# Fifteen matmuls that nothing reads, a load moved behind the weights and a unit moved between two steps, at the start of a Fourier filter with a mixture of experts

## The chip, the core and the metric

The kernel runs on one core of a Trainium2 chip. A core has a matrix engine (TensorE, PE in the rows), a vector engine (VectorE, DVE), a scalar engine (ScalarE, ACT), a general engine (GpSimd, POOL) and a sync engine (SyncE, SP), which here does little but start transfers; 16 DMA engines carry the transfers. The metric is the time of one execution in microseconds, as the median of several runs; less is better.

## What is computed

For each of 8 sequences of 3136 rows and 256 columns: a real Fourier transform along the rows, a complex 256 x 256 matrix with a bias, a shrinking of small values to zero, the transform back; then, on the result, the 128 rows with the highest score go through a two-layer network whose output is added to them. Cut to what matters:

```python
X = np.fft.rfft(x, axis=1)
Yr = X.real @ w_r - X.imag @ w_i + b_r
Yi = X.real @ w_i + X.imag @ w_r + b_i
Yr = np.sign(Yr) * np.maximum(np.abs(Yr) - 0.01, 0.0)   # Yi likewise
y = np.fft.irfft(Yr + 1j * Yi, n=3136, axis=1)
for b in range(8):
    top = np.argpartition(-(y[b] @ w_gate), 128)[:128]
    ye = np.maximum(y[b, top] @ w1, 0.0) @ w2
    out[b, top] = y[b, top] + sigmoid(y[b, top] @ w_gate)[:, None] * ye
```

## The kernel before

The transform of length 3136 is split as 49 x 64, and so is every batch's work.

- **First stage**, `s1(b, i)`, i from 0 to 7 (a unit): a load of 512 KB of x (`ld_x`), four matmuls of 49 x 64 on 512 columns each that fill the four quarters of the array, and two copies out, one on ACT (L430), one on DVE (L431). For b > 0 the result goes to DRAM as `As[b]` (512 KB). Batch 0 is split: the even rows of each unit go to `early` (256 KB, `st_a(i, 0)`), the odd rows later to `late` (`st_a(i, 1)`).
- **Second stage**, `s2(b, g)`, g from 0 to 12 (a step of a batch): four matmuls of 128 x 128 on the tile `av` and the constants `g_sb` into the one PSUM buffer `px`; then `Xh`, `Xl`, a split of the result in two parts, by ACT (L466, L467), DVE (L468) and POOL (L469). `ld_a` loads `av` from `early`, `late` or `As` for two steps at a time in two transfers of 256 KB.
- **Spectral stage**, `spectral(b, g, p)`: twelve matmuls of 256 columns for each p of 0 and 1 (L221 to L223), then the shrinking (L490, L492, L497) and a split (L504, L505).
- **Back**: `s2i`, a store of its result, `ld_c`, `s1i`, and the score and network in threads between the steps.

The main loop runs over t, the count of steps of all batches. Step t does, in this order on TensorE, `s2` of step t+1, the first half of `spectral` of step t, `s2i` of step t-2, the second half, and then units of `s1` of later batches where the list `first` has them due: units 2 and 3 of batch 1 in step 2, 4 and 5 in step 4. `s2` of batch 0 is written (0,0), (0,1) and so on below.

Order is fixed by hand: `ordered` ties each instruction to the one before it on PE, ACT, DVE and SP; `ld` ties each load on SP to the load before it (`queued`). So an instruction on TensorE that waits holds up all that stand behind it there, and the transfers that SP starts go out in the order of the program. `flush` starts the stores that have gathered since the last step.

Ahead of the main loop stands a part of its own: the eight loads of batch 0, the eight units with their stores to `early`, one load and unit of batch 1, the weights `w_r` and `w_i` with their split (`split_w`), the first `av`, the second load of batch 1, further constants, and the stores to `late`. Its unit (1,1) stands in step 0 of the loop, behind `s2` (0,1).

Of the kernel before, what the change touches and what calls it, by code (L numbers as in the profile page):

```python
# [10 lines left out]
F32 = mybir.dt.float32  # L11
# [6 lines left out]
ALU = mybir.AluOpType  # L18

B, S, D = 8, 3136, 256  # L20
# [85 lines left out]
def fourier_moe(ctx: ExitStack, tc: tile.TileContext, x, w_r, w_i, bri, wg, w1, w2,  # L106
                t_wf, t_wq, t_g, t_gi, t_m, t_dig, outs, cap):
    nc = tc.nc
# [3 lines left out]
    pool = ctx.enter_context(tc.tile_pool(name="work", bufs=2))  # L112
    ps = ctx.enter_context(tc.tile_pool(name="ps", bufs=2, space=bass.MemoryType.PSUM))
# [6 lines left out]
    def c_tile(shape, dt, name):  # L120
        return const.tile(shape, dt, name=name)

    w1f, w1tf = c_tile([128, 64], F32, "w1f"), c_tile([128, 64], F32, "w1tf")
    w1p = c_tile([128, 64], F32, "w1p")
    nc.scalar.dma_start(out=w1p, in_=t_wf[2])
    nc.scalar.dma_start(out=w1f, in_=t_wf[0])
    early, late = [dram.tile([2, 32, N2, 128], F32, name=n, bufs=1) for n in ("early", "late")]
    last = {}
    g_sb = c_tile([128, NJ, 128], F32, "g_sb")
# [19 lines left out]
    def queued(eng, f):  # L149
        if eng in last:  # L150
            with tc.issue_after(last[eng]):
                last[eng] = f().ins
        else:
            last[eng] = f().ins

    def ld(out, src):
        queued(nc.sync, lambda: nc.sync.dma_start(out=out, in_=src))
# [4 lines left out]
    def ld_w(src, name, bufs):  # L162
        t = pool.tile([128, 2, D], F32, name=name, bufs=bufs)
        ld(t, src.rearrange("(h p) e -> p h e", p=128))
        return t

    def split_w(t, h, l):
        nc.vector.tensor_copy(h, t)
        nc.vector.tensor_tensor(out=l, in0=t, in1=h.bitcast(F32), op=ALU.subtract)

    def add_bias():
        nc.vector.tensor_scalar(out=bias, in0=bias, scalar1=LAM, scalar2=None, op0=ALU.add)
        nc.vector.memset(m2l, -2.0 * LAM)

    def consts_g(k):
        s = slice(4 * k, min(4 * k + 4, NJ))
        ld(g_sb[:, s, :], t_g[:, s, :])

    def ld_gi(k):
        s = slice(4 * k, min(4 * k + 4, NJ))  # L180
        t = pool.tile([P, 8, 128], F32, name="cv", bufs=4)[:, :s.stop - s.start, :]
        ld(t, t_gi[:, s])
        gis.append((t, s))
# [7 lines left out]
    def consts_b():  # L191
        ld(wq, t_wq)
        ld(w1tf, t_wf[1])
        make_identity(nc, ident)
# [205 lines left out]
    def store(dst, src):  # L400
        if t < ORD:
            nc.sync.dma_start(out=dst, in_=src)
        else:
            stores.append((dst, src))

    def flush():
        for dst, src in stores:
            nc.sync.dma_start(out=dst, in_=src)
        stores.clear()
        done["s1i"] = done["last"]  # L410

    def tiles4(out, w, src):
        for r in (1, 0):
            for c in range(2):
                last_mm = nc.tensor.matmul(out[r][64 * c:64 * c + 64], w[64 * r:64 * r + N1, :], src(r, c), start=True, stop=True)  # L415
        return last_mm.ins

    def ld_x(b, i):
        xt[b, i] = pool.tile([P, 4, D], F32, name="cv" if b == 0 and i >= 4 else "xt", bufs=4)
        ld(xt[b, i], x[b, i])  # L420

    def s1(b, i):
        if i == 0:
            As[b] = dram.tile([2, 64, N2, 128], F32, name="As")
        n = ("at", "at", "at", "ct", "ct", "ot", "ot", "ot")[i] if b == 0 else "cv" if b == 1 and i < 2 else "at"
        a = pool.tile([P, 8, 128], F32, name=n, bufs={"ct": 2, "cv": 4}.get(n, 3))
        p = [ps.tile([P, 4, 128], F32, name="s", bufs=4) for _ in range(2)]
        xi = xt.pop((b, i))
        tiles4(p, w1f if b else w1p, lambda r, c: xi[64 * r:64 * r + N1, :, 128 * c:128 * c + 128])
        nc.scalar.copy(out=a[:, :4, :], in_=p[0])  # L430
        nc.vector.tensor_copy(a[:, 4:, :], p[1])  # L431
        if b > 0:
            store(As[b].rearrange("h q n d -> (h q) n d")[:, 8 * i:8 * i + 8, :], a)
        else:
            made.append(a)
# [3 lines left out]
    def st_a(i, k):  # L439
        ld((early, late)[k].rearrange("h q n d -> (h q) n d")[:, 8 * i:8 * i + 8, :], made[i][k::2])  # L440

    def pads(h):
        ld(As[0][h, N1:].rearrange("p (i n) d -> i p (n d)", n=8), x[0, :, 64 * h + N1:64 * h + 64].rearrange("i p m d -> i p (m d)"))
# [126 lines left out]
    PE, ACT, DVE, SP = [getattr(mybir.EngineType, n) for n in ("PE", "Activation", "DVE", "SP")]  # L570
# [65 lines left out]
    def ordered(f, *args, engines=()):  # L636
        bb = nc.cur_bb.bb.instructions
        n = len(bb)
        f(*args)
        for i in bb[n:]:  # L640
            if i.engine in (engines or (PE, ACT, DVE, SP)):
                if i.engine in chain:
                    tc.add_manual_dep(i, chain[i.engine].name, mybir.DependencyInfo(
                        mybir.DependencyClass.NoSync, mybir.DependencyReason.DATA), reason="main order")
                chain[i.engine] = i

    def at_step(u, f, n, kind=None):
        if 0 <= u < B * G:
            for i in range(-(-(u * n) // G), -(-((u + 1) * n) // G)):
                if t < ORD:  # L650
                    f(*divmod(i, n))
                else:
                    ordered(f, *divmod(i, n))
                if kind and i % n == n - 1:
                    done[kind] = i // n
# [7 lines left out]
    def to_step(u, f):  # L663
        todo = unloaded if f is ld_c else left
        while len(todo) > B * U - units_by(u):
            b, i = todo[0]
            ordered(f, b, i)
            if f is s1i and i == U - 1:
                done["last"] = b
# [7 lines left out]
    def firsts(u):  # L677
        for i in first:
            if first[i] == u:
                ordered(s1, *divmod(i, U))  # L680

    def loads(u):
        for n in range(1 if u < 0 else U):
            i = loaded[0]
            if u < -AP or i == B * U or first[i] > u + XP or sum(first[k] >= u for k in range(U + 2, i)) > 3:
                break
            ordered(ld_x, *divmod(i, U))
            loaded[0] += 1

    t = -1  # L690
    for i in range(U):
        ld_x(0, i)
    consts_g(0)
    for i in range(U):
        s1(0, i)
        st_a(i, 0)
        if i == 1:
            ld_x(1, 0)
    ws = [ld_w(w_r, "r1", 1), ld_w(w_i, "Yl", YB)]
    s1(1, 0)  # L700
    split_w(ws[0], wrh, wrl)
    split_w(ws[1], wih, wil)
    ld_a(0, 0)
    ld_a(0, 1)
# [12 lines left out]
    for t in range(-1, B * G):  # L717
        if t > 0:
            at_step(t + AP, ld_a, G)
        loads(t)  # L720
        to_step(t + 2, ld_c)
        if t < ORD:
            flush()
        else:
            ordered(flush)
        if t >= 0 and t % 2 == 0 and (t + 4) // 2 in range(2, 7):
            consts_g((t + 4) // 2)
        if t % 2 and (t + 3) // 2 in range(2, 7):
            ld_gi((t + 3) // 2)
        if t == 10:  # L730
            consts_b()
        if t in (14, 16):
            pads((t - 14) // 2)
        if t in range(20, 20 + 2 * (FF // 128 + 2), 2):
            consts_moe((t - 20) // 2)
        at_step(t + 1, s2, G)
        if t == 0:
            ordered(s1, 1, 1)
            add_bias()
        at_step(t - 1, shrink_c, G)  # L740
        tick(threads)
        at_step(t, lambda b, g: spectral(b, g, 0), G)
        if t == B * G - 1:
            at_step(t, shrink_a, G)
            at_step(t, shrink_b, G)
            at_step(t, shrink_c, G)
        at_step(t - 2, s2i, G)
        if t == B * G - 1:
            at_step(t - 2, gate, G, "s2i")
            break  # L750
        at_step(t, lambda b, g: spectral(b, g, 1), G)
        at_step(t, shrink_a, G)
        firsts(t)
        at_step(t - 2, gate, G, "s2i")
        at_step(t, shrink_b, G)
        if t < B * G - 2:
            to_step(t, s1i)
        if t == 0 or t % 2 and (t + 1) // 2 in range(1, 7):
            ordered(consts_gi, *gis.pop(0))
        if t in range(28, 28 + 2 * (FF // 128), 2):  # L760
            ordered(split_w2, (t - 28) // 2)
        tick(threads)
        if main_pe[0] is not None:
            with tc.issue_after(main_pe[0]):
                ticks[0] += 1
                tick(ffns)
# [80 lines left out]
```

## Time and profile before

| | us |
|---|---|
| median of 3 runs | 702.11 |
| lowest and highest of them | 702.02, 702.75 |
| profiled execution, its own time | 703.28 |
| profiled execution, span from first to last instruction | 701.5 |

The rows further down come from the one profiled execution: its 703.28 us are 701.5 of span and 1.8 around it. Times in rows are counted from the first instruction. PE is busy 670.2 us of the span. A matmul of 128 x 256 in fp32r takes one record, one in f32 two; a unit of `s1` gives 8 records, `s2` of a step gives 8. TensorE's clock has two levels, 1.2 and 2.4 GHz; PEclk 0.50 is the first and 1.00 the second. The row of PEclk says 1.00 from the span's start on, before its first change is recorded.

### The profile page before, as it was taken

The numbers are of one execution on the slowest core, as the hardware profiler recorded it, in microseconds if no ns is written. First come the engines' busy times: TensorE is split into PE (matmuls) and PEld (weight loads), VectorE is DVE, ScalarE is ACT, GpSimd is POOL, SyncE is SP. The second block draws the span as 40 slices with busy tenths as digits, with TensorE's granted clock in tenths as the row PEclk, the third lists the DMA queues.
The fourth block names the chain that finished last, engine by engine and source line by source line (L and its number), as shares of the span: only waits on it lengthen the run. The fifth ranks groups of instructions, "written<-read, shape, count | busy, mean of one in ns | idle before, by whom it ended". The sixth has DMA issues, their size and how long they took to land.

```text
span 701.5 us, 15027 instructions
## 1 busy us (share of the span) xinstructions
PE 670.2 (96%) x5482; PEld 552.9 (79%) x5482; DVE 464.8 (66%) x1330; ACT 384.3 (55%) x759; POOL 209.5 (30%) x255
## 2 busy tenths in 40 slices
PE   6499999999999999999999999999999999998997
PEld 2288888989888988888888798788878888876666
DVE  2355666666665555555877877777997789866852
ACT  2255665655566666666566556655555454445441
POOL 1034342233333333222223232322323222232321
PEclk9699999999999999999999999999999999999999
DMA  9999987787799999999899999887778665647950
GB/s 334 310 370 376 324 269 254 250 282 248 259 346 340 332 329 317 338 309 334 283 333 329 304 321 333 279 308 256 240 217 254 207 214 186 198 154 217 388 229 23
DMA packets 146791, 196.31 MB, mean 280 GB/s; under 512 B 8725, under 2 KB 111278, under 8 KB 146718
## 3 DMA queue, kind: packets, MB, share of 16 engines
q1 hardware_dynamic: 145518, 193.08, 81.8%
q0 software_dynamic: 912, 2.21, 1.0%
q8 instruction: 43, 0.70, 0.4%
q14 instruction: 30, 0.25, 0.1%
q10 hardware_dynamic: 288, 0.07, 0.0%
HBM read 101.59 MB, written 94.83 MB: 280 GB/s over the span
## 4 chain that ended last, share of the span: by engine, by line
PE 79%; DVE 11%; issue 4%; DMA 3%; ACT 2%; POOL 0%; SPq 0%; POOLq 0%; DVEq 0%; ACTq 0%
PE s L415 16%; PE px L463 12%; PE py L221 12%; PE py L222 12%; PE py L223 12%; PE s L221 3%; PE s L222 3%; PE s L223 3%; DMA av<-early 2%; DVE py L490 2%; DVE junk L536 2%; DVE yf L497 1%; PE py L369 1%; DVE Xl L468 1%; PE s L369 1%
## 5 line engine op out<-in xcount | busy, mean ns | idle before, releaser
L505 POOL TENSOR_TENSOR Yl<-yf,Yh 128x512 fp32r<-128x512 f32 (+1 forms) x104 | 130.6, 1255 | 331.6 <-ACT Yh L504 325.4
L492 ACT ACTIVATE r<-py,m2l 128x512 f32<-128x512 f32 (+1 forms) x104 | 69.8, 672 | 169.7 <-DVE py L490 165.1
L490 DVE TENSOR_TENSOR py<-py,bias 128x512 f32<-128x512 f32 (+1 forms) x104 | 70.3, 676 | 110.6 <-PE py L223 105.4
L463 PEld LDWEIGHTS px<-g_sb,av 128*128 128x128 f32 (+1 forms) x800 | 99.3, 194 | 40.2 <-DVE at L431 21.3
L463 PE MATMUL px<-g_sb,av 128*128 128x128 f32 (+1 forms) x800 | 114.7, 286 | 9.3 <-DMA av<-early 7.0
L221 PE MATMUL py<-wrh,Xh 128*128 128x256 f32 x400 | 122.2, 306 | 0.0
L223 PE MATMUL py<-wrl,Xh 128*128 128x256 f32 x400 | 112.7, 282 | 0.0
L222 PE MATMUL py<-wrh,Xl 128*128 128x256 f32 x400 | 112.6, 282 | 0.0
L221 PE MATMUL py<-wih,Xh 128*128 128x256 f32 x400 | 112.4, 281 | 0.0
L222 PE MATMUL py<-wih,Xl 128*128 128x256 f32 x400 | 112.1, 280 | 0.0
L223 PE MATMUL py<-wil,Xh 128*128 128x256 f32 x400 | 111.8, 279 | 0.0
L468 DVE TENSOR_TENSOR Xl<-px,Xh 128x512 fp32r<-128x512 f32 (+1 forms) x104 | 69.5, 668 | 34.0 <-ACT Xh L467 26.8
L536 DVE CUSTOM_DVE_ANT_0 junk<-ct,wgb 128x256 f32<-128x256 f32 (+1 forms) x200 | 86.5, 433 | 6.1 <-ACT ct L523 2.9
L523 ACT COPY ct<-s 128x512 f32<-128x512 f32 (+1 forms) x104 | 59.3, 571 | 51.6 <-PE s L223 50.2
L221 PEld LDWEIGHTS py<-wrh,Xh 128*128 128x128 f32 x400 | 75.9, 190 | 3.5 <-issue 2.3
L222 PEld LDWEIGHTS py<-wrh,Xl 128*128 128x128 f32 x400 | 76.0, 190 | 0.9 <-issue 0.9
L223 PEld LDWEIGHTS py<-wrl,Xh 128*128 128x128 f32 x400 | 75.8, 189 | 0.0
L221 PEld LDWEIGHTS py<-wih,Xh 128*128 128x128 f32 x400 | 75.5, 189 | 0.0
L222 PEld LDWEIGHTS py<-wih,Xl 128*128 128x128 f32 x400 | 75.4, 188 | 0.0
L223 PEld LDWEIGHTS py<-wil,Xh 128*128 128x128 f32 x400 | 75.3, 188 | 0.0
L466 ACT CAST Xh<-px 128x512 fp32r<-128x512 f32 (+1 forms) x104 | 59.6, 573 | 27.7 <-PE px L463 22.0
L497 DVE SCALAR_TENSOR_TENSOR yf<-py,r 128x512 f32<-128x512 f32 (+1 forms) x104 | 69.4, 668 | 6.6 <-ACT r L492 2.3
(129 smaller groups left out, 1201.1 us busy)
## 6 DMA issues: line engine op xcount, KB each, us to landing
xt<-in_x SPq DMA_DIRECT2D x60, 512.0 KB, 6.7
cv<-As SPq DMA_DIRECT2D x58, 512.0 KB, 5.5
out<-ot SPq DMA_DIRECT2D x57, 512.0 KB, 3.8
As<-at SPq DMA_DIRECT2D x54, 512.0 KB, 4.0
As<-ct SPq DMA_DIRECT2D x96, 256.0 KB, 4.7
av<-As SPq DMA_DIRECT2D x84, 256.0 KB, 4.9
out<-at SPq DMA_DIRECT2D x7, 512.0 KB, 7.7
xt<-As SPq DMA_DIRECT2D x6, 512.0 KB, 4.1
```

Of the source, the lines that this page charges most:

```text
L221: nc.tensor.matmul(out, wh, mh, start=start, stop=False)
L222: nc.tensor.matmul(out, wl, mh, start=False, stop=False)
L223: return nc.tensor.matmul(out, wh, ml, start=False, stop=stop).ins
L415: last_mm = nc.tensor.matmul(out[r][64 * c:64 * c + 64], w[64 * r:64 * r + N1, :], src(r, c), start=True, stop=True)
L463: nc.tensor.matmul(px[:, 2 * p + h, :], a[:, h, 2 * (g % 2) * (w - 1) + p, :], g_sb[:r, 2 * g + p, :], start=True, stop=True)
L466: nc.scalar.copy(out=xh[:, :, NF:], in_=px)
L468: nc.vector.tensor_tensor(out=xl[:, :, NF:], in0=px, in1=xh[:, :, NF:].bitcast(F32), op=ALU.subtract)
L490: nc.vector.tensor_tensor(out=p, in0=p, in1=bias[:, :w, :], op=ALU.add)
L492: nc.scalar.activation(out=r1[b, g], in_=p, func=AF.Relu, bias=m2l, scale=1.0)
L497: nc.vector.scalar_tensor_tensor(out=yf, in0=py.pop((b, g)), scalar=0.0, in1=r1.pop((b, g)), op0=ALU.min, op1=ALU.add)
L505: nc.gpsimd.tensor_tensor(out=yl, in0=yf, in1=yh.bitcast(F32), op=ALU.subtract)
L536: nc.vector.tensor_tensor_reduce(out=junk[:r], in0=c[:, k, :], in1=wgb[:r], scale=1.0, scalar=0.0, op0=ALU.mult, op1=ALU.add, accum_out=Cs ...
```

## The change

- `w1f`, the first-stage constant of batches 1 to 7 (32 KB), is loaded on SP behind the loads of batch 0 and `g_sb`, and not on ACT's queue at the start.
- A tile `busy` is filled with 0.5 by DVE, and four f32 matmuls of 128 x 256 on it stand ahead of batch 0's units on TensorE, eleven more behind them. Their result is read by nothing.
- The units of batch 0 and unit (1,0) are tied in order on TensorE.
- The load of unit (1,0) moves from behind batch 0's second store to behind the weights.
- The low parts of the split weights are made by POOL, and not DVE.
- Unit (1,1) moves from step 0 to step -1, between `s2` (0,0) and `s2` (0,1); its store is then in the next `flush`, one step earlier.
- `add_bias` is tied in order.

```diff
-    nc.scalar.dma_start(out=w1f, in_=t_wf[0])
...
     def split_w(t, h, l):
         nc.vector.tensor_copy(h, t)
-        nc.vector.tensor_tensor(out=l, in0=t, in1=h.bitcast(F32), op=ALU.subtract)
+        nc.gpsimd.tensor_tensor(out=l, in0=t, in1=h.bitcast(F32), op=ALU.subtract)
...
     consts_g(0)
+    ld(w1f, t_wf[0])
+    busy = pool.tile([128, 2, D], F32, name="yf")
+    nc.vector.memset(busy, 0.5)
+    unread = ps.tile([128, 2, 128], F32, name="m", bufs=1)
+
+    def keep_clock(n):
+        for _ in range(n):
+            nc.tensor.matmul(unread, busy[:, 0, :128], busy[:, 1, :].rearrange("p (a c) -> p a c", a=2), start=True, stop=True)
+
+    ordered(keep_clock, 4, engines=(PE,))
     for i in range(U):
-        s1(0, i)
+        ordered(s1, 0, i, engines=(PE,))
         st_a(i, 0)
-        if i == 1:
-            ld_x(1, 0)
+    ordered(keep_clock, 11, engines=(PE,))
     ws = [ld_w(w_r, "r1", 1), ld_w(w_i, "Yl", YB)]
-    s1(1, 0)
+    ld_x(1, 0)
+    ordered(s1, 1, 0, engines=(PE,))
...
         at_step(t + 1, s2, G)
+        if t < 0:
+            ordered(s1, 1, 1)
         if t == 0:
-            ordered(s1, 1, 1)
-            add_bias()
+            ordered(add_bias)
```

Where instructions stand now. On TensorE, from the start to the first spectral stage, before (`m` is the PSUM tile of the unread matmuls, `s` that of a unit, `px` that of `s2`, `py` that of `spectral`):

```order
L415 MATMUL s<-xt,w1p 64x512 x16
L415 MATMUL s<-cv,w1p 64x512 x16
L415 MATMUL s<-xt,w1f 64x512 x4
L463 MATMUL px<-g_sb,av 128x128 x8
L415 MATMUL s<-xt,w1f 64x512 x4
L221 MATMUL py<-wrh,Xh 128x256
```

and in the change:

```order
L700 MATMUL m<-yf 128x256 x4
L414 MATMUL s<-xt,w1p 64x512 x16
L414 MATMUL s<-cv,w1p 64x512 x16
L700 MATMUL m<-yf 128x256 x11
L414 MATMUL s<-xt,w1f 64x512 x4
L462 MATMUL px<-g_sb,av 128x128 x4
L414 MATMUL s<-xt,w1f 64x512 x4
L462 MATMUL px<-g_sb,av 128x128 x4
L220 MATMUL py<-wrh,Xh 128x256
```

Unit (1,1), the second `s<-xt,w1f`, has moved between the two `s2`, and the unread matmuls stand around batch 0's 32.

On SP, from the constants behind batch 0's loads to the first `av`, before:

```order
L157 DMA g_sb<-t_g 128x512
L157 DMA early<-at 64x1024 x2
L157 DMA xt<-in_x 128x1024
L157 DMA early<-at 64x1024
L157 DMA early<-ct 64x1024 x2
L157 DMA early<-ot 64x1024 x3
L157 DMA r_193<-in_w_r 128x2x256
L157 DMA Yl<-in_w_i 128x2x256
L157 DMA av<-early 128x4x128 x2
```

and in the change:

```order
L156 DMA g_sb<-t_g 128x512
L156 DMA w1f<-t_wf 128x64
L156 DMA early<-at 64x1024 x3
L156 DMA early<-ct 64x1024 x2
L156 DMA early<-ot 64x1024 x3
L156 DMA r_209<-in_w_r 128x2x256
L156 DMA Yl<-in_w_i 128x2x256
L156 DMA xt<-in_x 128x1024
L156 DMA av<-early 128x4x128 x2
```

One load of x, 512 KB, has moved behind six stores and the weights; the number of bytes ahead of `av` is the same but for `w1f`.

On SP some 25 transfers later, around the third pair of `av`, which is for `s2` (0,4) and (0,5); `As<-cv` is the store of a unit of batch 1. Before:

```order
L157 DMA xt<-in_x 128x1024
L408 DMA As<-cv 128x1024
L157 DMA xt<-in_x 128x1024 x3
L157 DMA g_sb<-t_g 128x512
L157 DMA av<-early 128x4x128 x2
L408 DMA As<-cv 128x1024
L157 DMA cv<-t_gi 128x512
```

and in the change:

```order
L156 DMA xt<-in_x 128x1024
L407 DMA As<-cv 128x1024
L156 DMA xt<-in_x 128x1024 x3
L407 DMA As<-cv 128x1024
L156 DMA g_sb<-t_g 128x512
L156 DMA av<-early 128x4x128 x2
L156 DMA cv<-t_gi 128x512
```

The store of unit (1,1) has moved ahead of a constant and the pair of `av`. Behind this place the order of every engine is that of before.

## Rows read from the trace of the kernel before

**Rows 1.** The page: busy time by engine, and the chain that ended last, by engine.

```profile
PE 670.2 (96%) x5482; PEld 552.9 (79%) x5482; DVE 464.8 (66%) x1330; ACT 384.3 (55%) x759; POOL 209.5 (30%) x255
...
PE 79%; DVE 11%; issue 4%; DMA 3%; ACT 2%; POOL 0%; SPq 0%; POOLq 0%; DVEq 0%; ACTq 0%
```

**Rows 2.** That chain in order of time, 0 to 60 us: start, us, what.

```profile
5.62 13.19 PE s L415 x64
...
19.44 3.51 DMA early<-ot
23.15 3.99 DMA av<-early
...
31.26 2.07 PE px L463 x8
33.33 1.92 PE s L415 x8
...
35.76 0.21 PE py L222
...
37.41 0.12 PE py L221
...
41.77 8.22 DMA av<-early
```

**Rows 3.** TensorE in order of time: start, us, what [idle before it, and releaser].

```profile
27.27 2.30 PE L463 MATMUL px<-g_sb,av 128*128 128x128 f32 x8 [6.84 <-DMA av<-early]
...
39.00 1.05 PE L463 MATMUL px<-g_sb,av 128*128 128x128 f32 x8
...
47.33 1.95 PE L415 MATMUL s<-xt,w1f 49*64 49x512 f32 x16
...
50.03 0.94 PE L463 MATMUL px<-g_sb,av 128*128 128x128 f32 x6 [0.17 <-DMA av<-early]
...
527.48 0.18 PE L271 MATMUL m<-n,tm 128*128 128x6 bf16 x1 [1.58 <-DVE idx L338]
```

**Rows 4.** Stretches: us, busy PE, PEld, DVE, ACT, POOL; PEclk, DMA share, GB/s.

```profile
23.00:24.00 1.00, 0.00 (x0) 0.00 (x0) 0.00 (x0) 0.00 (x0) 0.00 (x0) 0.77 0.21 73
24.00:25.00 1.00, 0.00 (x0) 0.00 (x0) 0.43 (x2) 0.00 (x0) 0.00 (x0) 0.50 0.59 178
...
37.00:38.00 1.00, 1.00 (x10) 1.00 (x9) 0.00 (x0) 0.00 (x0) 0.00 (x0) 0.90 1.03 395
...
49.00:50.00 1.00, 0.73 (x6) 0.30 (x2) 0.83 (x3) 0.95 (x2) 0.00 (x0) 1.00 1.04 404
```

**Rows 5.** VectorE in order of time, the copies out of batch 0's units.

```profile
14.46 0.69 DVE L431 COPY ct<-s 128x512 f32<-128x512 f32 x1 [1.01 <-PE s L415]
16.17 0.69 DVE L431 COPY ot<-s 128x512 f32<-128x512 f32 x1 [1.02 <-PE s L415]
17.39 0.69 DVE L431 COPY ot<-s 128x512 f32<-128x512 f32 x1 [0.53 <-PE s L415]
18.25 0.69 DVE L431 COPY ot<-s 128x512 f32<-128x512 f32 x1 [0.17 <-PE s L415]
```

**Rows 6.** SP in order of time: start, us, what it issues.

```profile
10.65 0.54 SPq L157 DMA_DIRECT2D xt<-in_x  x1
...
41.20 1.22 SPq L157 DMA_DIRECT2D av<-early  x2
42.53 1.76 SPq L408 DMA_DIRECT2D As<-cv  x1
```

**Rows 7.** All transfers from 36 to 50 us.

```profile
DMA packets 2617, 5.24 MB, mean 374 GB/s; under 512 B 228, under 2 KB 1307, under 8 KB 2617
```

**Rows 8.** The page's costliest groups: a subtraction of 128 x 512 on POOL.

```profile
L505 POOL TENSOR_TENSOR Yl<-yf,Yh 128x512 fp32r<-128x512 f32 (+1 forms) x104 | 130.6, 1255 | 331.6 <-ACT Yh L504 325.4
```

**Rows 9.** Stretches at the end, PE alone: us, busy PE, PEclk, DMA share, GB/s.

```profile
696.00:697.00 1.00, 0.77 (x7) 1.00 0.00 0
...
699.00:700.00 1.00, 0.00 (x0) 0.69 0.37 131
```

## The prediction

> **What bounds the kernel now.** I read the page first: PE is busy 96% of the span and holds 79% of the chain that ended last, DMA only 3% of it [rows 1]. So the end is set by how early TensorE gets into its unbroken work, and what a change at the start is worth is read from where the chain last leaves TensorE for something else. I then followed the chain in order of time [rows 2]. It goes through batch 0's units (13.19 us), the last store to `early` (19.44, 3.51 us to land), the first `av` (23.15, 3.99 us), `s2`, unit (1,1) and the first spectral matmuls, and then once more through a transfer: the pair of `av` whose second half was issued at 41.77 and took 8.22 us, up to 49.99. TensorE's own rows say the same: the last six records of `s2` (0,4) start at 50.03 and waited for `av` [rows 3]. The 3% of DMA in the chain, some 21 us, are the pieces up to here and the first load; behind 50 us no transfer is on the chain. The reader should see from this that there are two stretches: up to 50.03 the DMA queue decides, behind it TensorE's own work, 651.5 us of the 701.5.
>
> The clock is the third thing. PEclk falls in the stretch 23 to 24 us, mean 0.77, is 0.50 in the next, and comes back in 37 to 38, mean 0.90 [rows 4]. The spectral matmul at 35.76 takes 0.21 us of the chain, the one at 37.41 takes 0.12 [rows 2]. In the first stage the profile prints 1.00, but the copies out of the units follow each other after 1.71 us (14.46 to 16.17) and later after 0.86 us (17.39 to 18.25) [rows 5]: the first units ran at the low level too, until 16 or 17 us.
>
> **The change part by part.**
>
> *Unread matmuls.* The trace has none. The nearest row is `s2`: four f32 matmuls of 128 columns in 1.05 us at 39.00 and in 2.30 us at 27.27 [rows 3], so 256 columns cost 0.53 us at the high and 1.15 at the low level. Four ahead of batch 0 cost 2.1 to 4.6 us; they begin behind a fill of 128 x 512 on DVE, which I price as a copy, 0.69 us [rows 5], and TensorE's first matmul waits until 5.62 anyway [rows 2]. They are hidden, or push the first unit by some 0.3 us. Eleven behind it cost 5.8 to 12.6 us. TensorE stands still there for 6.84 us before `s2` (0,0) [rows 3]; at the high level they fit. At the low level they would run over by up to 6 us, and what hides that is the wait at 50 us, below.
>
> *First stage at the high clock, if the four raise it.* Eight units at 0.86 rather than 1.71 us are paced by the arrival of x. The last store to `early` is then issued up to 2 us before 19.44. It lands no earlier than the queue in front of it lets it.
>
> *Load of (1,0).* It leaves its place at 10.65 [rows 6], ahead of six stores to `early`, and goes behind the weights, ahead of `av`. One transfer of 512 KB (0.524 MB) at the 374 GB/s of a full queue [rows 7] is 1.40 us. So the stores can land up to 1.40 us earlier. But as many bytes as before go ahead of `av`, so `av` gains only what the queue stood idle: 0.79 us in 23 to 24 and 0.41 in 24 to 25 [rows 4], together **1.20 us**. Ends: 0 if the last store is issued no earlier (its 3.51 us stay), 1.40 if the whole transfer comes off. I take 1.20, since the idle stretch is a row and the moved load is what fills it. Every transfer behind `av` is issued in a full queue and gains the same.
>
> *Weights' low parts on POOL.* Two subtractions at 1.26 [rows 8], 2.5 us in a row, where DVE took two of 128 x 512 at about 0.69 each: 1.1 us more. The weights stand ahead of `av` in the queue, and the first spectral matmul comes 3.8 us or more behind `av`, so `s2` covers it: nothing. Without that cover it would be 1.1 us on TensorE, again inside the wait at 50 us.
>
> *w1f on SP, `add_bias` tied.* 32 KB in the queue is 0.09 us, and `w1f` is needed only at unit (1,0). The bias is ready long before its use. Nothing.
>
> *Unit (1,1) between the steps, with a clock kept up.* `s2` (0,1) starts 1.69 us after `s2` (0,0) ends (27.27 + 2.30 to 31.26), because `px` must be emptied. The unit fits into that: half of 1.95 [rows 3]. At the high level TensorE does `s2` (1.05), waits 1.69 with the unit in it, and does `s2` (1.05): 3.8 us from the landing of `av` to the first spectral matmul, where it now takes 8.0 (27.27 to 33.33 + 1.92). I allow 1.5 us for x of (1,1), which lands behind `av`; then TensorE is 1.2 + 8.0 - 5.3 = 3.9 us ahead, and the nine spectral matmuls up to 37.2 that took 0.21 rather than 0.12 give 0.8 more: **4.7 us ahead**.
>
> *What is late next.* `s2` (0,4). Its `av` is issued in a full queue (DMA share 1.03 and 1.04 in the stretches on either side, [rows 4]), so it lands when the bytes ahead of it are through. These are 1.20 us earlier, but the store of (1,1), issued at 42.53 behind this `av` [rows 6], now stands ahead of it: another 512 KB, **1.40 us**, later. Net: 49.99 - 1.20 + 1.40 = 50.19. TensorE arrives 4.7 us early, near 44.6 (it came at 47.33 + 1.95 = 49.28), and waits there; the units behind it, (1,2) and (1,3), are already done, and nothing can pass in its fixed order. All that TensorE won is given back.
>
> **Sum.** Against the profiled execution: span 701.5 - 1.20 + 1.40 = 701.7, its own time 703.28 + 0.2 = 703.5. The median of the runs lies 1.2 below that execution, so the forecast for the median is 702.11 + 0.2 = **702.3 us**. With the ends of the gain (1.40 and 0) it is 702.1 to 703.5; the upper end is rival C.
>
> **Rivals.**
>
> *A, slower: the clock falls in the new wait.* The wait at `s2` (0,4) is from 44.6 to about 49.5, some 5 us. Twice in this trace the clock fell when TensorE had stopped: 27.27 - 6.84 = 20.43 is the start of one stop, and the fall lies in 23 to 24; at the end the last matmuls run until about 696.8 and the fall lies in 699 to 700 [rows 9], so it came some 3 us into each. A stop of 1.58 us, at 527.48 [rows 3], left it at the high level. Five us is longer than both; the price is then paid where TensorE is the bound. Last time TensorE worked without a break from 31.26 to 37.2, 5.9 us, before the level came back, and half of that is lost: 2.95 us; if it comes back sooner, 1.5. That gives 702.3 + 2.7 = 705.0 (703.8 to 705.3). It decides from a stop of about 3 us on. Against it: the stop between the eleven matmuls and unit (1,0), near 3 us too, could make the clock fall first; then TensorE is some 2.5 us later at `s2` (0,4), the stop there shrinks to about 2.5, and nothing is lost. The Trainium skill, TensorE: Matmul & The Clock Gate, under Why this matters for your kernels, speaks against this change here: it says that idle gaps between bursts of matmuls send the engine back to the low clock. By that rule the time is that of this rival, 705.0; the trace agrees in its two long stops and has none of this size in its middle.
>
> *B, faster: the queue is not what holds `av` at 50 us.* If the store of (1,1) costs the pair nothing, the time is 702.1 - 1.2 = 700.9; if the pair also follows TensorE, all 4.7 us are kept: 697.4. For it: SP's own issue of three loads and the pair is spread over some 5 us ahead of 42.53, not at once. Against it: DMA shares of 1.03 and 1.04, and 8.22 us from issue to landing against 3.99 for the first `av` [rows 2].
>
> *C, the change doesn't do what it says:* four matmuls do not raise the clock, the units run at 1.71 us each, the last store goes out at 19.44 as before, and the gain of 1.20 is missing. The store of (1,1) still comes ahead: 702.1 + 1.4 = 703.5.
>
> **How the numbers follow.** About 0.2% (1.4 us) is what a measurement of this kernel can tell from no change. Forecast 0.46, with 701.7 to 703.2 as its own range (its lower end less the 0.4 by which single runs stray); A 0.28; B 0.14, of which only the full gain, 0.12, lies beyond 0.2%; C 0.12, half of it beyond. A ends beyond 0.2% nearly always. Faster 0.13, same 0.53, slower 0.34. For the range I leave out B's full gain at the low end and the worst of A at the high end, together under 0.2: 700.9 to 705.0.
>
> **What would show it.** Right: in the new profile the copies of batch 0's units follow each other at about the pace of x and the first `av` lands near 26; spectral work begins near 31 rather than 35; `s2` (0,4) waits several us for `av`, and its last six records start within 0.5 us of 50.2; the chain still holds that `av`. For A, PEclk falls between 45 and 50 and spectral matmuls behind it take 0.21. Wrong: `s2` (0,4) ends before 49.5 (B), or the first `av` lands at 27 again (C). The prediction falls as a whole if TensorE doesn't wait at `s2` (0,4) at all.

## The result, and the profile after

| | before | after |
|---|---|---|
| median, us (5 runs each, same chip) | 702.11 | 705.74 |
| lowest and highest | 701.92, 702.75 | 705.66, 706.56 |
| profiled execution, own time | 703.28 | 705.74 |
| its span | 701.5 | 703.9 |

The changed kernel is slower: ratio 1.0052, 95% interval 1.0037 to 1.0066, that is 3.63 us between the medians. The time lies outside the predicted range, 0.74 us above its upper end. What happened is rival A: the clock fell in the new wait at `s2` (0,4).

The page of the changed kernel, busy time by engine and the chain by engine, as in [rows 1]: TensorE is still busy 96% of the span, but 4.5 us longer, while the chain's share of DMA grew from 3 to 4%.

```profile
PE 674.7 (96%) x5512; PEld 557.6 (79%) x5512; DVE 464.8 (66%) x1329; ACT 384.3 (55%) x759; POOL 212.0 (30%) x257
...
PE 78%; DVE 10%; DMA 4%; issue 4%; ACT 2%; SPq 1%; POOL 0%; POOLq 0%; DVEq 0%; ACTq 0%
```

TensorE of the changed kernel in order of time, as in [rows 3] (`m` are the unread matmuls, one f32 matmul gives two records):

```profile
1.45 3.44 PE L700 MATMUL m<-yf 128*128 128x256 f32 x8 [1.45 <-DVE f L248]
...
16.32 5.02 PE L700 MATMUL m<-yf 128*128 128x256 f32 x22
24.87 1.98 PE L414 MATMUL s<-xt,w1f 49*64 49x512 f32 x8 [3.53 <-DMA xt<-in_x]
...
28.80 1.09 PE L414 MATMUL s<-xt,w1f 49*64 49x512 f32 x8
...
37.93 1.16 PE L462 MATMUL px<-g_sb,av 128*128 128x128 f32 x8
42.53 1.95 PE L414 MATMUL s<-xt,w1f 49*64 49x512 f32 x16
49.13 2.41 PE L462 MATMUL px<-g_sb,av 128*128 128x128 f32 x8 [4.64 <-DMA av<-early]
56.79 1.05 PE L462 MATMUL px<-g_sb,av 128*128 128x128 f32 x8
```

The reader is to see three things. TensorE comes to `s2` (0,4) at 42.53 + 1.95 = 44.48, where it came at 49.28 before. It waits there 4.64 us for `av`. And this `s2` takes 2.41 us, where the same eight records took 1.05 at 39.00 before: the low level.

Stretches of the changed kernel, columns as in [rows 4]; the last three figures of a row are PEclk, DMA share and GB/s:

```profile
24.00:25.00 1.00, 0.13 (x4) 0.16 (x8) 0.68 (x1) 0.00 (x0) 0.64 (x2) 0.95 1.03 308
...
28.00:29.00 1.00, 0.86 (x9) 0.69 (x11) 0.00 (x0) 0.31 (x1) 0.00 (x0) 0.85 1.00 343
...
48.00:49.00 1.00, 0.00 (x0) 0.00 (x0) 0.00 (x0) 0.00 (x0) 0.00 (x0) 0.89 1.07 355
49.00:50.00 1.00, 0.87 (x3) 0.62 (x3) 0.00 (x0) 0.00 (x0) 0.00 (x0) 0.50 1.14 315
...
55.00:56.00 1.00, 1.00 (x8) 1.00 (x8) 0.00 (x0) 0.59 (x1) 0.00 (x0) 0.69 0.99 404
```

The clock falls at 24.9, at the end of the stop of 3.53 us ahead of unit (1,0), and is back at 28.3, where before it was low from 23.5 to 37.2. It falls again at 48.8, while TensorE waits for `av` and is busy 0.00 of the stretch, and comes back at 55.6. The Trainium skill, TensorE: Matmul & The Clock Gate, section Why this matters for your kernels, says that idle gaps between bursts of matmuls throw the clock back; in this wait of 4.64 us the trace agrees.

The chain of the changed kernel in order of time, as in [rows 2]:

```profile
19.71 5.03 DMA xt<-in_x
...
39.71 9.28 DMA av<-early
...
49.13 2.41 PE px L462 x8
51.54 0.21 PE py L220
...
55.78 0.12 PE py L222
```

The pair of `av` for `s2` (0,4) is on the chain again, this time with its first half, up to 48.99, and the spectral matmuls behind it take 0.21 us each until 55.8. SyncE, as in [rows 6], shows the store of unit (1,1), `As<-cv`, now ahead of that pair:

```profile
19.71 0.41 SPq L156 DMA_DIRECT2D xt<-in_x  x1
...
38.70 0.42 SPq L407 DMA_DIRECT2D As<-cv  x1
...
39.71 1.01 SPq L156 DMA_DIRECT2D av<-early  x2
```

**Where the time went.** From the start of `s2` (0,5) to the end the two profiled executions are alike: 701.5 - 54.34 = 647.2 us before, 703.9 - 56.79 = 647.1 after. So all of the difference is the start of `s2` (0,5), 2.45 us later. From the start of `s2` (0,4) to that of `s2` (0,5) it is 56.79 - 49.13 = 7.66 us now; with the clock up it is 4.31 us from the last six records to the next step (54.34 - 50.03), plus 0.62 for the first two. The fall therefore costs 7.66 - 4.93 = **2.7 us** (0.17 of the 4.93 is a wait for the second half of the pair), and the pair landed at nearly the old time (its last packet at 49.84, before at 49.99). The other 1.2 us of the 3.63 is no loss in the rows: the profiled execution of before lay 1.17 above its own median, that of after lies on its own.

### The profile page after: what moved, and what is told of

It is laid out like the page before. It is cut to its first block, busy times and chain, and to the rows that moved or that the text cites. A ratio compares the mean times of both kernels' runs of the same rounds, so it can differ in the third digit from the quotient of the medians.

```text
span 703.9 us, 15092 instructions
## 1 busy us (share of the span) xinstructions
PE 674.7 (96%) x5512; PEld 557.6 (79%) x5512; DVE 464.8 (66%) x1329; ACT 384.3 (55%) x759; POOL 212.0 (30%) x257
## 4 chain that ended last, share of the span: by engine, by line
PE 78%; DVE 10%; DMA 4%; issue 4%; ACT 2%; SPq 1%; POOL 0%; POOLq 0%; DVEq 0%; ACTq 0%
PE s L414 14%; PE py L220 12%; PE px L462 12%; PE py L221 12%; PE py L222 12%; PE s L220 3%; PE s L221 3%; PE s L222 3%; DMA cv<-in_x 1%; DVE py L489 1%; DVE junk L535 1%; PE py L368 1%; DMA av<-early 1%; DVE Xl L467 1%; PE s L368 1%
```

## The experiments

The medians below were taken on several chips, each beside the kernel before on the same chip (its median stands in the last column), so ratios are what is to be compared. Columns: when TensorE comes to `s2` (0,4) in the profiled execution, how long it waits there, when `s2` (0,5) starts, in which stretch of 45 to 60 us the clock was low, the span, the median, the ratio with its interval, and the median of before.

| kernel | comes | waits | `s2` (0,5) | low in 45 to 60 | span | median | ratio | before |
|---|---|---|---|---|---|---|---|---|
| before | 49.28 | 0.3 | 54.34 | no | 701.5 | 702.11 | | |
| after | 44.48 | 4.64 | 56.79 | 48.8 to 55.6 | 703.9 | 705.74 | 1.0052 (1.0037, 1.0066) | 702.11 |
| e0 | 48.39 | 0.3 | 53.43 | no | 700.6 | 702.80 | 0.9992 (0.9978, 1.0005) | 702.88 |
| e5 | 45.37 | 4.70 | 56.50 | 47.0 to 53.9 | 705.2 | 705.73 | 1.0035 (1.0015, 1.0054) | 702.56 |
| e14 | 47.23 | 1.45 | 53.44 | no | 700.7 | 705.65 | 1.0044 (1.0030, 1.0058) | 702.23 |
| e8 | 45.91 | 4.30 | 57.84 | 49.7 to 56.6 | 705.0 | 706.67 | 1.0056 (1.0039, 1.0073) | 702.56 |
| e11 | 47.28 | 0 | 51.79 | no | 700.5 | 702.13 | 0.9992 (0.9980, 1.0005) | 702.54 |
| e4 | 45.54 | 2.31 | 52.61 | no | 701.2 | 704.90 | 1.0026 (1.0010, 1.0042) | 702.56 |
| e2 | 46.84 | 0.94 | 52.52 | no | 699.7 | 702.71 | 1.0000 (0.9985, 1.0015) | 702.88 |
| e3 | 46.63 | 0 | 51.14 | no | 698.8 | 701.89 | 0.9985 (0.9965, 1.0005) | 702.88 |
| e10 | 48.41 | 0 | 52.93 | no | 701.2 | 702.77 | 1.0008 (0.9985, 1.0030) | 702.54 |
| e1 | 46.31 | filled | 55.16 | no | 702.3 | 705.01 | 1.0025 (1.0015, 1.0036) | 702.88 |
| e6 | 44.28 | 1.84, rest filled | 53.32 | no | 702.0 | 704.06 | 1.0029 (1.0012, 1.0045) | 702.56 |
| e13 | 45.91 | filled | 54.05 | no | 701.7 | 704.34 | 1.0029 (1.0016, 1.0042) | 702.23 |
| e9 | 43.84 | 0.90 | 49.50 | no | 699.5 | 701.83 | 0.9991 (0.9977, 1.0005) | 702.54 |
| e12 | 46.92 | 0 | 51.43 | no | 700.3 | 699.96 | 0.9954 (0.9937, 0.9972) | 703.34 |

### Which part of the change loses the time

**e0**, the kernel before itself:

> The kernel before, profiled once more: the profile of before lay 1.2 us above the median of its runs, that of the changed kernel did not. Theory 1: the excess sits ahead of 50 us, where the transfers of that profile came late: in this profile the pair of av lands near 49.0 rather than 49.99 and the span is near 700.4. Rival: the excess lies behind 50 us: s2 (0,4) ends again at 50.97 and the span differs elsewhere.

Its `s2` (0,5) starts 0.9 us earlier than in the first profile of before, with nothing changed. So the arrival of transfers strays by at least 0.9 us, and the first profile was a late one. **e5**, the changed kernel itself, shows the wait and the fall again in another execution:

> The changed kernel as it is, on the same chip as the three below, so that they can be compared. In all profiles so far the span is the start of s2 (0,5) plus 647.2 us. Theory 1: the pair of av lands near 49 to 50, TensorE waits 3 us or more there, PEclk falls in the wait, s2 (0,5) starts near 56.8 and the span is near 704. Rival (the fall was that of one execution): in this profile the clock stays up, s2 (0,5) starts near 54.2 and the span is near 701.4.

TensorE of e5 in order of time:

```profile
50.07 2.40 PE L462 MATMUL px<-g_sb,av 128*128 128x128 f32 x8 [4.70 <-DMA av<-early]
56.50 1.05 PE L462 MATMUL px<-g_sb,av 128*128 128x128 f32 x8
```

**e8**, the kernel before with nothing but unit (1,1) and its store moved:

```diff
         at_step(t + 1, s2, G)
-        if t == 0:
+        if t < 0:
             ordered(s1, 1, 1)
+        if t == 0:
             add_bias()
```

> The kernel before with unit (1,1) between s2 (0,0) and s2 (0,1) and, with it, its store ahead of the pair of av; nothing else is changed. Theory 1 (queue order decides): the pair lands 1.3 us later than in before (49.1 to 50.0 there), near 50.8, TensorE waits 1 to 3 us for it, and the time is 1.3 us above before, ratio 1.0018. Rival (the store's place does nothing): ratio 1.000 or less.

TensorE of e8 in order of time:

```profile
43.96 1.95 PE L415 MATMUL s<-xt,w1f 49*64 49x512 f32 x16
50.21 2.44 PE L463 MATMUL px<-g_sb,av 128*128 128x128 f32 x8 [4.30 <-DMA av<-early]
57.84 1.05 PE L463 MATMUL px<-g_sb,av 128*128 128x128 f32 x8
```

The stretch of e8 in which its clock falls:

```profile
49.00:50.00 1.00, 0.00 (x0) 0.00 (x0) 0.00 (x0) 0.00 (x0) 0.00 (x0) 0.87 1.07 363
```

The moved unit alone gives the wait, the fall and the whole loss (1.0056). That is more than was expected of it, 1.3 us (1.0018) without a fall: the pair landed about where it should, its last packet at 50.96, but TensorE waited 4.30 us and not 1 to 3. **e11** is the complement, the change without the moved unit:

```diff
-        if t < 0:
-            ordered(s1, 1, 1)
         if t == 0:
+            ordered(s1, 1, 1)
             ordered(add_bias)
```

> The changed kernel with unit (1,1) and its store back in step 0; unread matmuls, moved load, weights on POOL stay. Theory (the moved unit with its store is the whole loss): the store of (1,1) is behind the pair again, which lands some 1.4 us earlier than in the changed kernel, near 48.4; TensorE comes later, since the unit stands behind s2 (0,1) and the pair waits no more than 2.5 us; no fall at 45 to 50, median within 1 us of before. Rival (the unread matmuls and the moved load lose by themselves): a fall at 45 to 50 here too, s2 (0,5) past 56, median 2.5 us or more above before.

There is neither wait nor fall, and no loss. **e4** keeps the moved unit and leaves out the fifteen unread matmuls (`keep_clock` with 0 rather than 4 and 11; the computation is whole):

> The changed kernel without its fifteen unread matmuls; everything else is as changed. Theory 1 (the unread matmuls only bring TensorE to the pair of av early, and the store of (1,1) delays that pair by 1.3): batch 0's units run at the low level, TensorE comes to s2 (0,4) later and waits 3 us or less, the clock stays up there, and the time is about 1 us above that of before: 703 to 704. Rival (the fifteen matmuls are what costs): the time is that of before or less, ratio 1.000 or below.

Its profiled execution (703.0) shows no fall at `s2` (0,4), but its ten runs stand in two groups, four at 701.9 to 703.3 and six at 704.9 to 705.9. The median, 704.90, lies above the 703 to 704 expected, so the loss is there without the unread matmuls (1.0026), and with them but without the moved unit it is not (e11): they are not its cause.

### Which path: the store ahead of the pair of `av`

**e2** puts the store of (1,1) back behind the pair, everything else as changed:

```diff
             ordered(s1, 1, 1)
+            late_store = stores.pop()
         if t == 0:
+            stores.append(late_store)
```

> The changed kernel with the store of unit (1,1) back behind the pair of av of s2 (0,4); the unit itself stays where the change has it. Theory 1 (queue order decides when the pair lands): the pair lands 1.3 us earlier, near 48.5, s2 (0,4) waits 3.3 us instead of 4.64; if the clock doesn't fall in that, 705.74 - 1.3 - 2.4 = 702.0, if it does, 704.4. Rival (the store's place does nothing, the pair lands when TensorE's progress or SP's issue lets it): s2 (0,4) starts near 49.1 and the time is 705.7.

TensorE of e2 in order of time:

```profile
47.19 0.46 PE L462 MATMUL px<-g_sb,av 128*128 128x128 f32 x2 [0.35 <-DMA av<-early]
48.23 0.94 PE L462 MATMUL px<-g_sb,av 128*128 128x128 f32 x6 [0.59 <-DMA av<-early]
52.52 1.05 PE L462 MATMUL px<-g_sb,av 128*128 128x128 f32 x8
```

The chain of e2:

```profile
39.43 8.76 DMA av<-early
```

The last six records start at 48.23, and the loss is gone in the median of ten runs (1.0000). The pair's last packet landed at 48.19 here and at 49.84 in the changed kernel, 1.65 us apart. This is near the 1.40 of the prediction, but no measure of it: the same packet landed at 50.78 in e5 and at 49.09 in e14, both the changed kernel. Steadier is the time from issue to landing of the pair's second half: 8.22 us in before, 8.46 in e0 and 8.76 in e2, with the store behind it; 9.62 in the changed kernel, 9.86 in e5, 9.23 in e14 and 9.73 in e8, with the store ahead. (e4 is an exception: 8.60 with the store ahead.) The Trainium skill, DMA: Bandwidth & Descriptors, section Queues, rings and completion order, says that descriptors on one ring are consumed in ring order; the longer time with the store ahead agrees.

The profile of e2 is not the store alone: the clock was low from 27.2 to 34.0, TensorE came at 46.84 rather than 44.48, and so the stop was 0.94 us and not the 3.3 expected. That the loss hangs on the store's place is shown by the medians of e2, e8 and e11 together.

**e3** goes further: the pair and its constant are issued ahead of two loads and that store.

```diff
             loaded[0] += 1
+            if i == U + 3:
+                ordered(consts_g, 2)
+                ordered(ld_a, 0, 4)
...
-        if t > 0:
+        if t > 1:
             at_step(t + AP, ld_a, G)
...
-        if t >= 0 and t % 2 == 0 and (t + 4) // 2 in range(2, 7):
+        if t > 0 and t % 2 == 0 and (t + 4) // 2 in range(2, 7):
             consts_g((t + 4) // 2)
```

> The changed kernel with the constants and the pair of av for s2 (0,4) issued behind the load of unit (1,3), ahead of the loads of (1,4) and (1,5) and of the store of (1,1). Theory 1 (TensorE is some 4.6 us ahead and only the queue order in front of this pair takes it back, and then the clock): the pair lands near 45 to 46, s2 (0,4) waits under 1.5 us, PEclk stays up, and all is kept: 705.74 - 2.4 - 4 = 699.3 (698.5 to 700.0), faster than both kernels. Rival (something else behind it, another transfer, a buffer or another engine, is late next): TensorE waits elsewhere in 45 to 65 us and the time is 702 or more.

The pair landed by 45.3, but TensorE came only at 46.63: the clock had been low from 27.1 to 33.9. It is a gain of at most 0.35% (interval 0.9965 to 1.0005) or none; 699.3 us was expected and 701.89 measured. **e10**, the same order of transfers in the kernel before, gains nothing that can be measured, as TensorE comes at 48.41 there:

> The kernel before with one edit: the same pair of av and its constant issued behind the fourth load of x of batch 1, ahead of two loads; no unread matmuls and no moved unit. Theory (before, TensorE and the pair come to s2 (0,4) within 0.7 us of each other, so an earlier pair alone wins only that): TensorE comes at about 48.5 to 49.3 and no longer waits, s2 (0,5) starts 0.5 to 1.0 us earlier than in before, no fall of the clock at 45 to 50, median 0.5 to 1.0 us below before, within 0.2%. Rival (the queue's order alone is worth as much as order and change together): median about 1.5 to 2.5 us below before, and the run with pair first in the changed kernel owes nothing to the change.

So an earlier pair is worth nothing that can be measured where TensorE doesn't come earlier too; whether both together are worth something, e3 doesn't show.

### What the fall in the wait costs

**e1** fills the wait with ten matmuls on `g_sb` that nothing reads, ahead of `s2` (0,4); **e6** with five, **e13** with eight:

```diff
+        if t == 3:
+            held = ps.tile([128, 2, 128], F32, name="m", bufs=1)
+            ordered(lambda: [nc.tensor.matmul(held, g_sb[:, 0, :], g_sb[:, 0:2, :], start=True, stop=True) for _ in range(10)], engines=(PE,))
         at_step(t + 1, s2, G)
```

> The changed kernel with ten more matmuls that nothing reads (128x256 f32, on the constants g_sb) ahead of s2 (0,4) on TensorE, in the wait of 4.64 us in which PEclk fell. Theory 1 (the fall in that wait costs 2.4 us, the pair of av is not touched): PEclk stays 1.00 from 30 us on, s2 (0,4) starts near 49.1 as in the changed kernel, s2 (0,5) near 54.2 instead of 56.79, time 705.74 - 2.4 = 703.3. Rival (the fall is a by-product, the time is lost by the later av or behind it): 705.7. If ten matmuls run past the landing of av: up to 0.3 us more than theory 1.

> The changed kernel with five unread matmuls (128x256 f32 on g_sb, 2.3 us) ahead of s2 (0,4), half of the ten that ran past the landing of av. Theory 1 (the fall in the wait is 2.4 to 2.7 us of the loss): the stop that is left is 2.3 us or less, PEclk stays up from 35 us on, s2 (0,5) starts 4.3 to 4.5 us after the landing of the pair, near 54.2, and the time is 2.4 less than that of the changed kernel on this chip. Rival (the clock in the wait costs nothing, work behind it is bound by another engine): the time is that of the changed kernel.

> The changed kernel with eight matmuls of 128 x 256 on g_sb, read by nothing, ahead of s2 (0,4): at 0.456 us each they take 3.65 us of the wait of 4.64, where five left a stop of 1.5 us and ten ran 1.6 us past the pair. Theory (the fall in the wait costs 2.6 us and is the larger part of the loss; the rest is the pair that lands 0.8 us later): no fall between 45 and 56 us, s2 (0,5) near 53.5, median 2 to 3 us below that of the changed kernel on this chip and within 1.4 us of before. Rival (the fall costs little of the time, since the queue holds what comes behind s2 (0,5) too): no fall, but a median within 1 us of the changed kernel's.

TensorE of e6 in order of time:

```profile
44.28 2.43 PE L747 MATMUL m<-g_sb 128*128 128x256 f32 x10
48.23 0.46 PE L462 MATMUL px<-g_sb,av 128*128 128x128 f32 x2 [1.52 <-DMA av<-early]
49.01 0.94 PE L462 MATMUL px<-g_sb,av 128*128 128x128 f32 x6 [0.32 <-DMA av<-early]
53.32 1.05 PE L462 MATMUL px<-g_sb,av 128*128 128x128 f32 x8
```

With five the clock stays up and `s2` (0,5) starts 3.2 us earlier than in e5. Of this, 1.8 us are the pair, whose last packet landed at 48.97 in e6 and at 50.78 in e5. So the price of the fall is better counted from that packet. With the clock up, `s2` (0,5) starts 4.33 to 4.35 us behind it in before, e0, e2, e4, e6 and e14. With the fall it is 6.95 us in the changed kernel (49.84 to 56.79), 6.88 in e8 (50.96 to 57.84) and 5.72 in e5 (50.78 to 56.50). The fall costs 2.6, 2.5 and 1.4 us in these three executions.

The medians gain 1.7 us in e6 and 1.3 in e13, each against the changed kernel on its chip, and the intervals overlap; neither the 2.4 us expected of e6 nor the 2 to 3 of e13 were reached. In e1 the ten ran until 50.89, past the pair at 49.15, since TensorE came later there; its median is 705.01, where 703.3 was expected. Unread work in a wait whose length strays either leaves a stop or delays what it was to protect. And all three, with no fall in the wait in their profiles, still lie 1.5 to 2.1 us above before by the medians, their intervals above 1. So the fall is a part of the loss, and these runs don't show that it is all of it.

**e14**, the changed kernel once more, happened to show it without the fall in the wait:

> The changed kernel itself, beside the one with eight matmuls in the wait. Theory: a stop over 4 us at s2 (0,4), a fall of the clock in it or at its end, s2 (0,5) near 56.6, median 2.5 to 4 us above before. Rival: the fall is missing in part of the runs, and the median lies within 1.5 us of the kernel with the eight matmuls.

Its nine runs stand in two groups, two at 702.5 and 702.6, seven at 705.2 to 707.0, and the profiled one is of the first. TensorE of it in order of time:

```profile
24.25 1.21 PE L414 MATMUL s<-xt,w1f 49*64 49x512 f32 x8 [3.35 <-DMA xt<-in_x]
...
45.28 1.95 PE L414 MATMUL s<-xt,w1f 49*64 49x512 f32 x16
48.38 0.46 PE L462 MATMUL px<-g_sb,av 128*128 128x128 f32 x2 [1.15 <-DVE Csc L535]
49.13 0.94 PE L462 MATMUL px<-g_sb,av 128*128 128x128 f32 x6 [0.30 <-DMA av<-early]
53.44 1.05 PE L462 MATMUL px<-g_sb,av 128*128 128x128 f32 x8
```

Two stretches of e14, in which the clock falls and comes back:

```profile
25.00:26.00 1.00, 0.51 (x5) 0.07 (x1) 0.53 (x1) 0.47 (x1) 0.37 (x1) 0.55 1.00 283
...
35.00:36.00 1.00, 1.00 (x9) 1.00 (x9) 0.18 (x2) 0.00 (x0) 0.44 (x1) 0.83 1.08 426
```

Here the clock is low first from 25.1 to 35.3 rather than to 28.3. TensorE comes 2.75 us later, the stop at `s2` (0,4) shrinks to 1.45 us, the clock does not fall in it, and the kernel takes what before takes (702.23 on this chip). The row names DVE as the releaser of the first 1.15 us; the first half of the pair landed at 48.24, just ahead of 48.38. This is the case by which the prediction set rival A aside. In the other profiles of the changed kernel (after, e5) the first fall is short, 3.4 us in each, and the second follows. The two kinds of run lie 705.8 (the middle one of the seven) - 702.6 = 3.2 us apart on one chip. The runs that were not profiled are put to the two kinds by their times alone.

### Where a kept lead goes

**e9** takes e3 and puts eighteen instead of eleven unread matmuls behind batch 0, so that the stop ahead of unit (1,0) is filled:

```diff
-    ordered(keep_clock, 11, engines=(PE,))
+    ordered(keep_clock, 18, engines=(PE,))
```

> The changed kernel with two edits: the pair of av for s2 (0,4) and (0,5) and its constant are issued behind the fourth load of x of batch 1, ahead of two loads and the store of unit (1,1), and eighteen instead of eleven unread matmuls stand behind batch 0's units, so that TensorE has no stop of 3.5 us ahead of unit (1,0). Theory (what the change lacked was a pair of av that comes as early as TensorE; a level that stays high to s2 (0,4) keeps its lead): no fall between 20 and 35 us, TensorE reaches s2 (0,4) between 44.5 and 45.5, where the pair has landed (45.3 in the run with the pair first alone), s2 (0,5) starts near 50, span near 697.3 (start of s2 (0,5) plus 647.2), median about 3 us below the kernel before. Rival (the early fall isn't what makes TensorE come at 46.6 when the pair is first, or the eighteen run past the landing of x): s2 (0,5) at 51 or later, span 698.5 or more, median at most 1.5 us below before.

The first half came true: PEclk is 1.00 in every stretch from 14 to 72 us, TensorE comes at 43.84, earlier than was expected, `s2` (0,5) starts at 49.50, 3.9 us ahead of e0. But the span is 699.5, not 49.50 + 647.2 = 696.7, and the median 0.7 us below before is not clear of noise. Most of the rest, 2.34 of 2.8 us, went to a third transfer. TensorE of e9 in order of time:

```profile
80.27 1.16 PE L462 MATMUL px<-g_sb,av 128*128 128x128 f32 x8 [2.34 <-DVE Xl L467]
```

ACT of e9 in order of time:

```profile
77.52 0.59 ACT L429 COPY at<-s 128x512 f32<-128x512 f32 x1 [4.08 <-DMA As<-at]
```

The chain of e9:

```profile
68.69 8.73 DMA As<-at
```

A copy out of a unit of batch 2 waits until 77.4 for a store to leave the buffer `at`; ACT and DVE stand still behind it for 4 us, and TensorE for 2.34. **e12** gives units (1,6) and (1,7) the buffers `ot`, free at that time:

```diff
-        n = ("at", "at", "at", "ct", "ct", "ot", "ot", "ot")[i] if b == 0 else "cv" if b == 1 and i < 2 else "at"
+        n = ("at", "at", "at", "ct", "ct", "ot", "ot", "ot")[i] if b == 0 else "cv" if b == 1 and i < 2 else "ot" if b == 1 and i > 5 else "at"
```

> The kernel of the run before with pair of av first and eighteen unread matmuls, and one edit: the results of units (1,6) and (1,7) are copied into the buffers called ot, free at that time, and not at, so that the copy of a unit of batch 2 no longer waits for the landing of the store As<-at that was issued at 68.69 and landed at 77.4. Theory (TensorE's lead of 3.9 us at s2 (0,5) was given back at that one store, which held up ACT and DVE and through them TensorE for 2.34 us at 77.9): that stop is gone, TensorE has no stop over 0.5 us between 50 and 90 us, span near 697.0, median about 3 us below the kernel before. Rival (the queue is full up to 90 us, so the next transfer takes the lead back in its place): a stop of 1.5 us or more for another transfer between 75 and 95 us, span 698.5 or more, median within 1.5 us of before.

This one beats the kernel before: ratio 0.9954 (0.9937 to 0.9972), 3.4 us by the medians. The changed kernel was not run on its chip, but had ratios of 1.0035 to 1.0052 on others. The stop at 77.9 is gone; TensorE has no stop from 36 to 97 us. The profiled execution took 702.03, longer than the median, and has two falls, from 28.6 to 35.4 and from 643.0 to 646.4; two stretches of it:

```profile
28.00:29.00 1.00, 0.28 (x4) 0.32 (x8) 0.69 (x1) 0.00 (x1) 0.18 (x1) 0.80 0.93 305
...
643.00:644.00 1.00, 1.00 (x10) 0.22 (x3) 0.18 (x1) 0.36 (x2) 0.00 (x0) 0.50 0.99 192
```

The four shortest of its twelve spans are 696.3 to 697.5 us, about the 697.0 that the theory asked for.

## Why the prediction was wrong

**Right.** What bounds the kernel, and where: behind `s2` (0,5) nothing changed, 647.2 and 647.1 us. The lead of TensorE, 4.7 us, arriving near 44.6: it came at 44.48, 4.8 earlier. That the number fits so well is luck in part: e5 against e0 gives 48.39 - 45.37 = 3.0, and the lead was reckoned with the clock up, which was low from 24.9 to 28.3. Its first term, 1.20 us at the first `av`, can't be told from stray: that transfer landed at 25.58 where it had landed at 27.14, but at 26.02 in e0 and 26.62 in e5. The four unread matmuls took 3.44 us between the bounds of 2.1 and 4.6; the eleven took 5.02 at the high level, less than the lower bound of 5.8 (0.46 us for one, where 0.53 was taken from `s2`). Batch 0's units then follow x; their copies, as in [rows 5], come 1.28 us apart in VectorE's order of time:

```profile
13.40 0.69 DVE L430 COPY ot<-s 128x512 f32<-128x512 f32 x1 [0.58 <-PE s L414]
14.68 0.69 DVE L430 COPY ot<-s 128x512 f32<-128x512 f32 x1 [0.59 <-PE s L414]
```

The split on POOL costs two subtractions of 1.26 us, as [rows 8] had it, and is hidden; POOL in order of time:

```profile
23.13 1.26 POOL L168 TENSOR_TENSOR wrl<-r,wrh 128x512 fp32r<-128x512 f32 x1 [20.32 <-DVE wrh L167]
24.76 1.26 POOL L168 TENSOR_TENSOR wil<-Yl,wih 128x512 fp32r<-128x512 f32 x1 [0.36 <-DVE wih L167]
```

The store ahead of the pair was to cost 1.40 us. From issue to landing the pair's second half took 9.2 to 9.9 us with it and 8.2 to 8.8 without, in the profiles named at e2, with e4 as the exception. The pair landed at 49.84, forecast 50.19, which is inside what that landing strays by. Rival B (the queue is not what holds `av`) falls, since TensorE waits for that pair in the changed kernel, in e5 and in e8; so does C (the clock is not raised), since the eleven matmuls ran at the high level.

**The step that failed** is the one that set A against the forecast: that the stop between the eleven matmuls and unit (1,0) "could make the clock fall first; then TensorE is some 2.5 us later at `s2` (0,4), the stop there shrinks to about 2.5, and nothing is lost". By this step the sum put the clock behind the new wait at nothing. The fall came first, as written (24.9), but its length was taken from the one long fall in the trace of before, [rows 4], and in two of three profiles of the changed kernel it lasts 3.4 us. TensorE then loses little, keeps its lead, stands 4.64 us (4.70 in e5) and the clock falls a second time, on the path, where it costs 2.6 us (1.4 in e5). e14 shows that the step describes a case that exists, in its profiled run and, by its time, in one more of nine; it was given 0.46 of the chance, and A 0.28. Nor does a long first fall always save the rest. In e13 the clock was low from 22.7 to 32.9 and TensorE still came at 45.91, where eight unread matmuls then filled 3.7 us; in e8, with the moved unit alone, low from 22.4 to 32.7, it came at 45.91 too, stood 4.30 us, and the clock fell again. Nothing in the trace of before said how long a first fall lasts when matmuls had run up to the stop, and the prediction did not hold that open.

**A term that was mis-sized.** A's price, 2.7 us, taken between 1.5 and 2.95 without a working, was 2.6 to 2.7 in the profiled execution. But A's sum ended at 705.0, since the forecast was carried from the profiled execution (703.28) to the median (702.11) by taking 1.2 off. Against the execution itself A gives 703.28 + 0.2 + 2.7 = 706.2; measured 705.74. Taking 1.2 off assumed that the changed kernel would lie below its own profile as before did. e0 shows what most of the 1.2 can have been: transfers ahead of 50 us that landed late in that one execution, 0.9 us of it at `s2` (0,5). The range's upper end, 705.0, was A's own value, though A itself went up to 705.3. What lies above A's value and B's 0.12 are together some 0.26 of the chance, and not under 0.2 as the prediction says.

**Left open.** Why the first fall lasts 3.4 us in some executions of one kernel and 10.2 in another; no run told that. How the loss is shared between the second fall and the later landing of the pair: e1, e6 and e13 take the fall away in the wait and keep 1.5 to 2.1 us of loss. Also the 1.1 us that e10 loses behind `s2` (0,5), and some 0.5 in e3 and e13, were not followed.

## What to carry to other kernels

A transfer that is issued one step earlier on a full queue delays what now stands behind it; before work is moved forward, look at which wait its store will stand in front of. If an engine gains a lead that the queue cannot follow, price the wait that arises not only at its own length but also with the lower clock behind it, where TensorE is the bound. And to move a prediction from a profiled execution to a median, ask first where that execution was late: its excess is not a constant of the kernel.

## What the runs showed of the hardware

- **The mean granted clock does not tell what a fall costs.** It is 0.993 in the profiled execution of the changed kernel (span 703.9) and 0.993 in e14's (700.7). The one was low 3.4 and 6.8 us, the second time behind the wait at `s2` (0,4), where it delayed all that followed. The other was low 10.2 us in one piece, ahead of a wait for a transfer that landed at 49.09.
- **No single length of stop divides the stops with a fall from those without.** e6 and e4 stood 1.5 and 2.0 us at `s2` (0,4) and stayed at the high level; in e12 the clock fell at 28.6 with 1.62 us as the longest stop since the unread matmuls.
- **A fall without a stop to match.** In five of the sixteen profiles (e4, e5, e6, e11, e12) the clock is low for some 3.4 us between 642 and 652, with TensorE at work, and the span is then 1.4 to 1.6 us longer than the start of `s2` (0,5) + 647.2. In each of the five it begins 1.8 to 2.2 us after the end of a stop of 1.2 us; the other eleven profiles have the same stop and no fall. It lengthens single runs, and no run shows that the change brings it: e5 has it, after and e14, the same kernel, have not.
